# Turning half of the token layer's input with VectorE block transposes and transfers instead of TensorE

## The chip, the cores and the metric

The kernel runs on one core of one Trainium2 chip. Its time is the device time of one execution in microseconds (us); lower is better. TensorE is called PE, its weight loads PEld, VectorE DVE, ScalarE ACT, GpSimd POOL, and SyncE, which issues nearly all DMA transfers here, SP. Each of them works through its own queue in order.

## The reference

Eight batch rows are computed, each by a thresholded attention over 8 heads (576 tokens, 64 channels a head) and then an MLP mixer. Everything is float32.

```python
def _attn_ref(q, k, v, tau):                      # q, k, v: (8, 8, 576, 64)
    scale = 1.0 / np.sqrt(q.shape[-1])
    scores = scale * np.matmul(q, k.transpose(0, 1, 3, 2))
    thresh = np.max(scores, axis=-1, keepdims=True) - tau
    scores = np.where(scores >= thresh, scores, -1000000000.0)
    scores = scores - np.max(scores, axis=-1, keepdims=True)
    attn = np.exp(scores)
    attn = attn / (np.sum(attn, axis=-1, keepdims=True) + 1e-09)
    return np.matmul(attn, v).astype(np.float32)

def _moe_ref(x, w_tok1, w_tok2, w_ch1, w_ch2):    # x: (8, 576, 512), the heads side by side
    xt = x.transpose(0, 2, 1)
    h = np.maximum(xt @ w_tok1, 0.0) @ w_tok2     # over tokens: 576 -> 256 -> 576
    u = x + h.transpose(0, 2, 1)
    h2 = np.maximum(u @ w_ch1, 0.0) @ w_ch2       # over channels: 512 -> 1536 -> 512
    return (u + h2).astype(np.float32)
```

## The kernel before, in words

**Attention.** The heads are taken in pairs, `pairs` (four a row), and pairs in quads of two: four heads, half of a row's 512 channels. A quad's tokens are cut into nine units of 128 scores' rows, 18 units a row; two units make a round. For a round PE computes the scores (L777), DVE the maxima (L794), POOL a bias from them (L800), ACT the threshold (L810) and the exponential with its sum (L820), DVE the inverse (L276, L277) and POOL the scaling (L285). The result `e` has to be turned before it can meet the values. In row 0 PE does that (L300). From row 1 on DVE turns blocks of 32x32 (L315, `turn_blocks`) and four transfers on SP put the blocks where they belong (L327, `move`). Three units form a group, for which PE multiplies by the values (L365, L370, `values`) into `xT`, the attention's output with channels on partitions: `xT` is 128 partitions x 4 pairs x 576 tokens. ACT or DVE copies it out of PSUM (L374).

**Token MLP.** `token_mlp(b)` builds its steps for a row when the row's last value group has been issued. The first token layer contracts over tokens, so x is needed with tokens on partitions, in `x_sb` (128 partitions x 5 token tiles x 512 channels, one buffer for all rows; the fifth tile has 64 tokens). `turn_x` transposes 128x128 blocks of `xT` on PE into a PSUM bank (L399), `turned_x` copies the bank to `x_sb` (L403, ACT, or DVE where that one is free first). `tok1` then multiplies with `w1`, five matmuls for each of the two blocks of 128 hidden channels (L411); L416 or L419 apply the relu. `tok2` (L424) is the second token layer, and `add_x` (L435) adds its result to `xT`, which from then on holds u. For row 0 the steps are made by half rows, `token_mlp(0, range(2))` as soon as its first quad is there.

**Channel MLP.** It works on groups of 256 tokens: `ch1` (L885, relu at L890 or L893) and `ch2` (L901, added to the turned u at L915 and stored at L925). Two groups of row 0 and one of each later row but the last are done while the attention of the next row runs; they are PE's filler there. What is left of u is spilled to DRAM (L483) and taken up at the end, from L1244 on, with no attention beside it.

**What sets the order.** The program is written out by a list scheduler at build time (`Scheduler`). Each operation has an engine, a cost, dependencies and a rank; the scheduler takes for each engine the operation that can start first by its own clocks and, among those that can start at once, the one of the lowest rank. Ranks: maxima -1 or 0, transfers of `e` 0, PSUM copies 0 or 1, token steps 1.5, channel steps 2, turns of `e` 4. Score rounds after row 0 are held back until the filler of a plan has been issued (`planned_at`, with `TOKENS` and `GROUP` as PE time of a row's token and channel work). Loads of q and k for a pair (`make_pair`, L106) have rank 0. During the attention PE shares two PSUM banks for everything but the scores. While the first 110 us of the scheduler's clock last, `keep_warm` (L599) fills PE's waits with spare transposes.

**Other names.** `extra` is a buffer of 4 KB a partition, which the conversion of the weights uses during rows 0 and 1 (`load_piece`, `converted`). `HQ`, in the new code, is 2, the pairs of a quad; `NI` is 4, `MAIN` 512 and `LAST` 64 tokens. `rows_due` holds rows whose token steps are to be made, `xreads` what must be finished before `xT`'s buffer is taken by the next row but one.

Of the kernel before, what the change touches and what calls it, by code (L numbers as in the profile page):

```python
# [21 lines left out]
def kernel(  # L22
# [356 lines left out]
    class Step:  # L379


        def __init__(self, kind, cost, on, cost_out, work, leave, other=None):
            self.kind, self.cost, self.on, self.cost_out, self.work, self.leave = kind, cost, on, cost_out, work, leave
            self.other = other

    def token_mlp(b, ps=range(NP)):

        xT = xTs[b]
        L = len(ps)
        cols = slice(P * ps[0], P * ps[0] + P * L)  # L390
        n = NI // L

        def turn_x(bank, t, n):
            M = MT[t]
            to = bank[0:M, 0 : n * L * P].rearrange("p (t c x) -> p t c x", t=n, c=L)
            for i in range(n):
                for c in range(L):
                    tok = (t + i) * P
                    nc.tensor.transpose(out=to[:, i, c, :], in_=xT[:, ps[c], tok : tok + M], identity=ident)  # L399

        def turned_x(bank, t, n, copy=nc.scalar.copy):
            M = MT[t]
            copy(  # L403
                out=x_sb[0:M, t : t + n, cols], in_=bank[0:M, 0 : n * L * P].rearrange("p (t c x) -> p t (c x)", t=n, c=L)
            )

        def tok1(bank, m):
            if b not in hidden:
                hidden[b] = work.tile([P, NTK, DM], F32, tag="a", bufs=1, name=f"a_{b}")
            for t in range(NT):  # L410
                nc.tensor.matmul(  # L411
                    bank[:, 0 : P * L], lhsT=w1[:, t, P * m : P * m + P], rhs=x_sb[:, t, cols], start=(t == 0), stop=(t == NT - 1)
                )

# [23 lines left out]
        for t, n in [(t, n) for t in range(0, NI, n)] + [(NI, 1)]:  # L438
            steps.append(
                Step(  # L440
                    "x",
                    0.115 * n * L,
                    "act",
                    0.49,
                    lambda bank, t=t, n=n: turn_x(bank, t, n),
                    lambda bank, t=t, n=n: turned_x(bank, t, n),
                    ("dve", 0.61, lambda bank, t=t, n=n: turned_x(bank, t, n, nc.vector.tensor_copy)),
                )
            )
# [70 lines left out]
    class Scheduler:  # L520
# [78 lines left out]
        def keep_warm(self, t):  # L599
# [3 lines left out]
            n = int((t - now - WARM_GAP) / WARM_TURN)  # L603
            if not banks or n < 1:
                return
# [121 lines left out]
    def make_pair(n):  # L727
        b, p = pairs[n]
        if n:
            ahead = (key_op("prep", n - 2, 0), key_op("prep", n - 2, 1))  # L730
            for lo in range(0, LOADS, 2):
# [6 lines left out]
                        ahead,  # L738
                        0,
                        after=(key_op("load", n - 1, LOADS - 2),),  # L740
# [97 lines left out]
    def make_tokens(b, steps, after):  # L838

        outs = {"x": [], "1": [], "20": [], "21": []}  # L840
        for i, step in enumerate(steps):
# [3 lines left out]
            elif step.kind == "1":  # L845
                deps += outs["x"] + tokens_x.get("2", []) + [key_op("pool", 0), key_op("pool", 1), key_op("pool", 2)]
            else:
                deps += outs["1"] + [key_op("pool", j) for j in range(3, 7)]
            x, y = put_step(("tok", b, id(step)), step, deps, b)
            outs[step.kind].append(y)  # L850
            fills[b] = fills.get(b, 0.0) + step.cost
        return outs

    state = {"ch2": [], "stores": [], "adds": []}

    def make_groups(b, halves):
# [124 lines left out]
    def make_row(b):  # L981
# [9 lines left out]
        outs = halves["20"] + halves["21"]  # L991
        xreads[b] = make_groups(b, halves) + outs
        if b < B - 1:
# [32 lines left out]
    def make_round(it):  # L1026
# [28 lines left out]
        for u in us:  # L1055
# [39 lines left out]
            if t % GU == GU - 1:  # L1095
                make_group(b, p0, t // GU)
                if p0 == NP - 2 and t // GU == 2:
                    rows_due.append(b)

    rows_due = []  # L1100

# [5 lines left out]

    TOKENS, GROUP = 18.8, 41.8

# [18 lines left out]
    def grow():  # L1128

        nonlocal made  # L1130
        while made < ROUNDS and (made < 2 or key_op("S", made - 2).end is not None):
            make_round(made)
            for n in range(2, len(pairs)):
                if last_round(n - 2) == made:
                    make_pair(n)
            made += 1
        if made > 4 and not first_half and key_op("V", 2).end is not None:
            make_half_row()
# [284 lines left out]
```

## Time and profile before

| | |
|---|---|
| median of 3 runs | 1273.56 us (1271.95 to 1276.34) |
| the profiled execution | 1275.34 us |
| its span, first to last instruction | 1273.5 us |
| granted TensorE clock, mean | 0.995 |
| busy: PE, PEld, DVE, ACT, POOL | 98%, 78%, 58%, 45%, 25% |
| turning transposes (L399) on PE | x160, from 76.7 to 865.8 us |
| first token layer (L411) on PE | x180 records: 140 of 512 columns, 40 of 256 |
| PE from the end of row 7's token phase on (905 to 1273.5 us) | 363.3 of 368.5 us busy |
| transfers of `e` (L327) | x504, 144 KB each, 2.9 us to landing |

A float32 matmul of the program stands in the trace as two records, a transpose as one. Busy times count overlapping records once; mean durations don't, and a matmul's end is modelled, so the distance between the starts of successive records says more of its cost than its duration. A line of a group reads: source line, engine, operation, what it writes and reads, shapes, count, then busy time and mean duration, then the idle time of its engine ahead of it and what ended it. A line of the timeline reads: start, length, engine, source line, operation, and in brackets the idle time before it.

### The profile page before, as it was taken

How to read it: one execution, taken by the hardware profiler on the slowest of the kernel's cores; microseconds unless marked ns; L12 is line 12 of the kernel's file. 1: busy time of each engine (PE TensorE's matmuls, PEld its weight loads, DVE VectorE, ACT ScalarE, POOL GpSimd, SP SyncE). 2: the span in 40 equal slices, each digit the busy share in tenths (PEclk: the TensorE clock that was granted, in tenths of full speed). 3: DMA queues.
4: the chain of work that ended last, by engine and by line, in shares of the span. 5: the costliest groups of instructions: out<-in, count | busy, mean ns of one | idle time of the engine just before them, and what ended most of it. 6: DMA issues, size and time to landing. Idle time of an engine off the chain costs nothing.

```text
span 1273.5 us, 21544 instructions
## 1 busy us (share of the span) xinstructions
PE 1244.8 (98%) x8090; PEld 993.5 (78%) x8090; DVE 744.7 (58%) x1145; ACT 570.7 (45%) x1244; POOL 316.9 (25%) x518
## 2 busy tenths in 40 slices
PE   8889999999999999999999999999999999999998
PEld 7656778687658767876876776787988888888887
DVE  6699982574666666765766667561443534444443
ACT  6988863663655565554565467431120202011120
POOL 3665641232223332332233333210001010000100
PEclk9899999999999999999999999999999999999999
DMA  8646985356877676677676676550111101020011
GB/s 161 143 123 166 226 197 122 79 128 154 174 155 168 144 154 148 149 161 160 157 150 152 153 158 157 129 130 11 52 24 66 34 25 42 18 67 25 25 34 33
DMA packets 307191, 145.09 MB, mean 114 GB/s; under 512 B 206672, under 2 KB 299856, under 8 KB 307088
## 3 DMA queue, kind: packets, MB, share of 16 engines
q1 hardware_dynamic: 305216, 143.51, 49.0%
q8 instruction: 64, 1.05, 0.3%
q10 hardware_dynamic: 1872, 0.21, 0.1%
q14 instruction: 39, 0.32, 0.1%
HBM read 47.32 MB, written 13.50 MB: 48 GB/s over the span
## 4 chain that ended last, share of the span: by engine, by line
PE 80%; DVE 6%; SPq 4%; DMA 3%; ACT 2%; issue 1%; POOL 0%; DVEq 0%; POOLq 0%
PE bank L901 12%; PE o L1244 10%; PE bank L885 10%; PE sc L777 9%; PE bank L370 8%; PE hx L1244 6%; PE bank L411 5%; PE bank L424 4%; PE hz L1244 4%; PE oz L1244 4%; PE hmm L1244 4%; DVE mx L794 3%; PE bank L365 2%; SPq L327 2%; DMA lv<-in_v_dram 1%
## 5 line engine op out<-in xcount | busy, mean ns | idle before, releaser
L285 POOL TENSOR_SCALAR e<-e,rr 128x576 f32<-128x576 f32 x288 | 213.7, 761 | 278.1 <-DVE rr L277 263.6
L810 ACT ACTIVATE e<-sc,bias 128x576 f32<-128x576 f32 x288 | 193.8, 740 | 149.5 <-POOL bias L800 146.3
L820 ACT ACTIVATE e<-e,ntau 128x576 f32<-128x576 f32 x288 | 220.5, 777 | 0.3
L794 DVE TENSOR_REDUCE mx<-sc 128x2 f32<-128x1152 f32 x144 | 187.9, 1345 | 48.3 <-PE sc L777 48.1
L315 DVE STREAM_TRANSPOSE T<-e 128x1152 f32<-128x1152 f32 x126 | 170.6, 1363 | 47.4 <-POOL e L285 24.3
L901 PEld LDWEIGHTS bank<-wc,g 128*128 128x128 f32 x1536 | 177.7, 192 | 9.8 <-issue 5.2
L901 PE MATMUL bank<-wc,g 128*128 128x128 f32 x1536 | 181.6, 276 | 0.4 <-DVE us L915 0.3
L885 PE MATMUL bank<-xT,wc 128*128 128x256 f32 x768 | 177.2, 384 | 1.1 <-DVE g L893 0.9
L777 PE MATMUL sc<-kT,qT 64*128 64x192 f32 (+1 forms) x1920 | 169.0, 338 | 2.7 <-ACT e L810 2.7
L777 PEld LDWEIGHTS sc<-kT,qT 64*128 64x128 f32 (+1 forms) x1920 | 141.0, 179 | 33.7 <-issue 17.7
L885 PEld LDWEIGHTS bank<-xT,wc 128*128 128x128 f32 x768 | 142.0, 190 | 29.0 <-issue 6.3
L370 PE MATMUL bank<-eT,lv 128*64 128x384 f32 (+1 forms) x1024 | 136.2, 408 | 0.0
L1327 POOL TENSOR_TENSOR us<-us,ut 128x256 f32<-128x256 f32 x27 | 22.5, 847 | 391.9 <-DVE us L1165 391.9
L370 PEld LDWEIGHTS bank<-eT,lv 128*64 128x64 f32 x1024 | 74.4, 138 | 51.4 <-issue 44.7
L800 POOL TENSOR_SCALAR bias<-mx,toff 128x2 f32<-128x2 f32 x144 | 39.4, 275 | 219.7 <-DVE mx L794 213.0
L411 PE MATMUL bank<-x_sb,w 128*128 128x512 f32 (+1 forms) x180 | 72.6, 552 | 0.3 <-DVE eT L305 0.2
L424 PE MATMUL bank<-w,a 128*128 128x192 f32 (+1 forms) x256 | 72.6, 418 | 0.1
L890 ACT ACTIVATE g<-bank 128x256 f32<-128x256 f32 x67 | 25.7, 383 | 91.2 <-PE bank L885 91.0
L1292 ACT ACTIVATE ga<-hmm 128x256 f32<-128x256 f32 x30 | 11.5, 383 | 117.1 <-PE hmm L1244 117.1
L1165 DVE TENSOR_TENSOR temps<-hx,temps 128x256 f32<-128x256 f32 x60 | 25.1, 418 | 56.7 <-PE hx L1244 56.6
L820 ACT ACTIVATION_READ_ACCUMULATOR e<-e,ntau 128x1 f32 x288 | 58.2, 202 | 0.0
L411 PEld LDWEIGHTS bank<-x_sb,w 128*128 128x128 f32 x180 | 33.1, 190 | 31.9 <-issue 29.8
(131 smaller groups left out, 1532.4 us busy)
## 6 DMA issues: line engine op xcount, KB each, us to landing
eT<-T SPq DMA_DIRECT2D x504, 144.0 KB, 2.9
lk<-in_k_dram SPq DMA_DIRECT2D x126, 72.0 KB, 3.0
lq<-in_q_dram SPq DMA_DIRECT2D x124, 72.0 KB, 3.1
out_dram<-us SPq DMA_DIRECT2D x32, 256.0 KB, 2.1
ut<-us SPq DMA_DIRECT2D x128, 64.0 KB, 2.1
lv<-in_v_dram SPq DMA_DIRECT2D x112, 72.0 KB, 2.5
spare<-in_moe_w_ch_dram SPq DMA_DIRECT2D x8, 512.0 KB, 3.6
extra<-in_moe_w_ch_dram SPq DMA_DIRECT2D x8, 512.0 KB, 3.9
```

What stands on the lines that cost most here:

```text
L285: nc.gpsimd.tensor_scalar(out=eh, in0=eh, scalar1=rr[:, h : h + 1], scalar2=1.0, op0=ALU.mult, op1=ALU.mult)
L315: nc.vector.transpose(out=T.rearrange("p a (c x) -> p c a x", c=NK), in_=e.rearrange("p (c a x) -> p c a x", c=NK, a=4))
L370: nc.tensor.matmul(to[r], lhsT=lv[:, j, :], rhs=e[j], start=False, stop=(c == NI - 1), skip_group_check=True)
L411: nc.tensor.matmul(bank[:, 0 : P * L], lhsT=w1[:, t, P * m : P * m + P], rhs=x_sb[:, t, cols], start=(t == 0), stop=(t == NT - 1))
L424: nc.tensor.matmul(bank[:, n * i : n * i + n], lhsT=hidden[b][:, m, P * c : P * c + P], rhs=w2[:, m, lo : lo + n], start=(m == 0), stop=(m ...
L777: nc.tensor.matmul(sc[h][rows, f, HT * k : HT * k + HT], lhsT=qT[r, cols], rhs=kT[r, HT * f : HT * f + HT], start=True, stop=True, skip_gr ...
L794: nc.vector.tensor_reduce(out=mx[:, h], in_=sc[h][:, :, 0 : 2 * HT].rearrange("p f (k x) -> p k f x", k=2), axis=AX.XY, op=ALU.max)
L810: nc.scalar.activation(out=eh, in_=part[h], func=AF.Prelu, bias=bias[:, h], scale=SCALE, alpha=STEEP)
L820: nc.scalar.activation(out=eh, in_=eh, func=AF.Exp, bias=ntau, accum_out=rs[:, h, 0:1])
L885: nc.tensor.matmul(bank[:, 0:n], lhsT=wc1[:, j, c, :], rhs=uT[:, c, GR * i : GR * i + n], start=(c == 0), stop=(c == NCC - 1))
L901: nc.tensor.matmul(to, lhsT=s["g"][:, j, P * t : P * t + P], rhs=wc2[:, j, P * c : P * c + P], start=(j == 0 and b > 0), stop=(j == NJ - 1 ...
L1244: nc.tensor.matmul(ps, lhsT=l, rhs=r, start=start and x == 0, stop=x == len(pairs) - 1, skip_group_check=not start)
```

## The change

From row 1 on the first quad's half of x no longer passes through PE. When the value group that ends the first quad has been issued, in mid-row, `make_early(b)` lays down: two turns on DVE (`turn_main`, one for each pair: 128 channels x 512 tokens by blocks of 32x32 into `extra`), four transfers on SP (`move_main`, each from 32 partitions of `extra` to 64 columns of all 128 partitions and four token tiles of `x_sb`), one more turn for the last 64 tokens (`turn_rest`) and four transfers for it (`move_rest`). The transfers wait for the turns and for the first token layer of the row before. The channels of this half stand in `x_sb` in another order, by blocks of 32, and `tok1` reads them back in the right one.

In `token_mlp` only the second quad is turned by PE: two groups of four transposes and one of two, where there were five groups of four. For that reason `tok1` makes two products of 256 columns in one bank in place of one of 512. Row 0 is made by half rows as before.

Besides, loads of q and k from pair 4 on get rank 1 instead of 0, `TOKENS` goes from 18.8 to 17.8, and `keep_warm` no longer acts while PE's clock is at 0, which drops the ten spare transposes before the first scores.

```diff
+    HQ = NP // 2
+
+    def early_x(b):
+        xT = xTs[b]
+        main = extra.bitcast(F32).rearrange("q (a t c d) -> q a t c d", a=4, t=NI, c=HQ)
+        rest = extra.bitcast(F32)[:, 0 : 2 * HQ * 32].rearrange("q (a c d) -> q a c d", a=2, c=HQ)
+        def turn_main(c):
+            nc.vector.transpose(
+                out=main[:, :, :, c, :].rearrange("q a t d -> q t a d"),
+                in_=xT[:, c, 0:MAIN].rearrange("q (t r a) -> q t a r", t=NI, a=4),
+            )
+        def turn_rest():
+            nc.vector.transpose(
+                out=rest.rearrange("q a c d -> q c a d"), in_=xT[:, 0:HQ, MAIN:S].rearrange("q c (r a) -> q c a r", a=2)
+            )
+        def move_main(i):
+            nc.sync.dma_start(
+                out=x_sb[:, 0:NI, 32 * HQ * i : 32 * HQ * i + 32 * HQ],
+                in_=main[32 * i : 32 * i + 32].rearrange("q a t c d -> q a (t c d)"),
+            )
+        def move_rest(i):
+            nc.sync.dma_start(
+                out=x_sb[0:LAST, NI, 32 * HQ * i : 32 * HQ * i + 32 * HQ],
+                in_=rest[32 * i : 32 * i + 32].rearrange("q a c d -> q a (c d)"),
+            )
+        return turn_main, turn_rest, move_main, move_rest
+
     def token_mlp(b, ps=range(NP)):
...
-        n = NI // L
+        turned = ps[HQ:] if b else ps
+        K = len(turned)
+        to_cols = slice(P * turned[0], P * turned[0] + P * K)
+        n = NI // K
...
         def tok1(bank, m):
...
-            for t in range(NT):
-                nc.tensor.matmul(
-                    bank[:, 0 : P * L], lhsT=w1[:, t, P * m : P * m + P], rhs=x_sb[:, t, cols], start=(t == 0), stop=(t == NT - 1)
-                )
+            if K == L:
+                products = [(cols, lambda t: x_sb[:, t, cols])]
+            else:
+                first = lambda t: x_sb[:, t, 0 : P * HQ].rearrange("p (i c d) -> p c i d", i=4, c=HQ)
+                products = [(slice(0, P * HQ), first), (to_cols, lambda t: x_sb[:, t, to_cols])]
+            for at, x in products:
+                to = bank[:, at.start - cols.start : at.stop - cols.start]
+                for t in range(NT):
+                    nc.tensor.matmul(
+                        to,
+                        lhsT=w1[:, t, P * m : P * m + P],
+                        rhs=x(t),
...
-            if not banks or n < 1:
+            if not banks or n < 1 or not now:
...
                         lambda lo=lo: load_qk(n, (nc.sync,) * 2, range(lo, lo + 2)),
                         ahead,
-                        0,
+                        1 if n >= NP else 0,
...
             elif step.kind == "1":
-                deps += outs["x"] + tokens_x.get("2", []) + [key_op("pool", 0), key_op("pool", 1), key_op("pool", 2)]
+                deps += outs["x"] + early.get(b, []) + tokens_x.get("2", []) + [key_op("pool", 0), key_op("pool", 1), key_op("pool", 2)]
...
+    def make_early(b):
+        turn_main, turn_rest, move_main, move_rest = early_x(b)
+        have = [key_op("X", rank_of_group(b, 0, g)) for g in range(3)]
+        free = early.get(b - 1, converted)
+        turns = [sched.op("dve", 1.1, lambda c=c: turn_main(c), have + free, 2) for c in range(HQ)]
+        before = [x for k, x in keyed.items() if k[0] == "tok" and k[1] == b - 1 and len(k) == 3 and x.first_layer]
+        moved = [sched.op("sp", 1.2, lambda i=i: move_main(i), turns + before, 0, dmas=(1, 131, 0.645)) for i in range(4)]
+        last = sched.op("dve", 0.35, turn_rest, moved, 2)
+        moved += [sched.op("sp", 0.6, lambda i=i: move_rest(i), [last] + before, 0, dmas=(1, 16, 0.6)) for i in range(4)]
+        early[b] = moved
+        xreads.setdefault(b, []).extend(turns + [last])
...
-    TOKENS, GROUP = 18.8, 41.8
+    TOKENS, GROUP = 17.8, 41.8
...
+        while early_due and key_op("V", rank_of_group(early_due[0], 0, 2)).end is not None:
+            make_early(early_due.pop(0))
```

More of the change, by code (lines that the diff above doesn't have):

```diff
@@ L390, in token_mlp @@
         cols = slice(P * ps[0], P * ps[0] + P * L)
-        n = NI // L
+        turned = ps[HQ:] if b else ps
+        K = len(turned)
+        to_cols = slice(P * turned[0], P * turned[0] + P * K)
+        n = NI // K
         def turn_x(bank, t, n):
             M = MT[t]
-            to = bank[0:M, 0 : n * L * P].rearrange("p (t c x) -> p t c x", t=n, c=L)
+            to = bank[0:M, 0 : n * K * P].rearrange("p (t c x) -> p t c x", t=n, c=K)
             for i in range(n):
-                for c in range(L):
+                for c in range(K):
                     tok = (t + i) * P
-                    nc.tensor.transpose(out=to[:, i, c, :], in_=xT[:, ps[c], tok : tok + M], identity=ident)
+                    nc.tensor.transpose(out=to[:, i, c, :], in_=xT[:, turned[c], tok : tok + M], identity=ident)
         def turned_x(bank, t, n, copy=nc.scalar.copy):
@@ L403, in turned_x @@
             copy(
-                out=x_sb[0:M, t : t + n, cols], in_=bank[0:M, 0 : n * L * P].rearrange("p (t c x) -> p t (c x)", t=n, c=L)
+                out=x_sb[0:M, t : t + n, to_cols], in_=bank[0:M, 0 : n * K * P].rearrange("p (t c x) -> p t (c x)", t=n, c=K)
             )
@@ L409, in tok1 @@
                 hidden[b] = work.tile([P, NTK, DM], F32, tag="a", bufs=1, name=f"a_{b}")
-            for t in range(NT):
-                nc.tensor.matmul(
-                    bank[:, 0 : P * L], lhsT=w1[:, t, P * m : P * m + P], rhs=x_sb[:, t, cols], start=(t == 0), stop=(t == NT - 1)
-                )
+            if K == L:
[10 more added lines that the diff above has]
+                        rhs=x(t),
+                        start=(t == 0),
+                        stop=(t == NT - 1),
+                        skip_group_check=len(products) > 1,
+                    )
         def relu(bank, m):
@@ L441, in token_mlp @@
                     "x",
-                    0.115 * n * L,
+                    0.115 * n * K,
                     "act",
@@ L849, in make_tokens @@
             x, y = put_step(("tok", b, id(step)), step, deps, b)
+            x.first_layer = step.kind == "1"
             outs[step.kind].append(y)
@@ L854 @@
     state = {"ch2": [], "stores": [], "adds": []}
+    early = {}
+    def make_early(b):
[9 more added lines that the diff above has]
+        xreads.setdefault(b, []).extend(turns + [last])
     def make_groups(b, halves):
@@ L991, in make_row @@
         outs = halves["20"] + halves["21"]
-        xreads[b] = make_groups(b, halves) + outs
+        xreads[b] = xreads.get(b, []) + make_groups(b, halves) + outs
         if b < B - 1:
@@ L1096, in make_round @@
                 make_group(b, p0, t // GU)
-                if p0 == NP - 2 and t // GU == 2:
-                    rows_due.append(b)
-    rows_due = []
+                if t // GU == 2:
+                    (rows_due if p0 == NP - 2 else early_due).append(b)
+    rows_due, early_due = [], []
     def planned_at(row, k):
```

## The prediction

> **What bounds the kernel now.** I read the page first: busy time and the slices.
>
> ```profile
> PE 1244.8 (98%) x8090; PEld 993.5 (78%) x8090; DVE 744.7 (58%) x1145; ACT 570.7 (45%) x1244; POOL 316.9 (25%) x518
> ...
> PE   8889999999999999999999999999999999999998
> ...
> DVE  6699982574666666765766667561443534444443
> ```
>
> PE is full from the fourth slice to the end; no other engine is near it. Since a busy PE need not be a limiting PE, I then cut the span at the first turning transposes of each row (rows 1 to 6 start theirs at 225, 346, 455, 557, 660 and 762 us) and looked at single stages.
>
> ```profile
> core 0: us, PE busy (x) PEld busy (x) DVE busy (x) ACT busy (x) POOL busy (x), PEclk, DMA share, GB/s
> 224.00:346.00 122.00, 119.73 (x888) 91.74 (x884) 75.18 (x98) 71.41 (x158) 34.92 (x62) 1.00 0.60 134
> 346.00:455.00 109.00, 106.05 (x767) 79.47 (x764) 68.17 (x100) 58.48 (x126) 33.75 (x58) 0.98 0.71 159
> 455.00:557.00 102.00, 101.08 (x747) 76.53 (x747) 68.69 (x98) 57.04 (x123) 30.48 (x54) 1.00 0.68 152
> 557.00:660.00 103.00, 102.72 (x762) 78.42 (x759) 67.95 (x98) 56.71 (x123) 30.22 (x54) 1.00 0.70 156
> ```
>
> PE idles 2.3, 3.0, 0.9 and 0.3 us of these stages and VectorE about a third of each. So PE work taken out of a row shortens the row, and work given to VectorE or to the transfers is free until it makes PE wait. What PE waits for now (list of waits, 224 to 906 us):
>
> ```profile
> PE bank L365 <- DVE xT L435: 2.5, 1, 2.5
> PE bank L365 <- DMA lq<-in_q_dram: 1.6, 1, 1.6
> PE bank L365 <- DMA eT<-T: 0.9, 1, 0.9
> ```
>
> The five lines below these name the short ones; the whole list is 7.5 us. The two longest are single halts, where the order of the work happens to fall badly.
>
> **Step 1, transposes removed from PE.** A row has 20 now (16 of 128 columns wide, 4 for the last 64 tokens), in five groups of four, each with one PSUM eviction at L403; it will have 10, in groups of 4, 4 and 2. Seven rows: 70 fewer transposes, 14 fewer groups. The mean duration of one (279 ns) isn't what it costs, since they overlap. Row 1's timeline on PE:
>
> ```profile
> 225.52 0.66 PE L399 MATMUL bank<-ident,xT 128*128 128x128 f32 x4
> 226.02 1.89 PE L885 MATMUL bank<-xT,wc 128*128 128x256 f32 x8
> 227.75 0.60 PE L399 MATMUL bank<-ident,xT 128*128 128x128 f32 x4
> 228.63 1.99 PE L885 MATMUL bank<-xT,wc 128*128 128x256 f32 x8 [0.28 <-DVE g L893]
> ```
>
> From the start of a group to the start of what follows is 0.50 us in the first and 0.88 us in the second, where what follows waits for a bank. Single starts lie 0.109 us apart. I added start-to-next-start over all 35 groups of rows 1 to 7: 3.4, 3.2, 3.5, 2.9, 3.3, 2.8 and 2.2 us, 21.2 us, or 0.607 us a group. At that price the new row costs 2 x 0.607 + (0.607 - 2 x 0.109) = 1.60 us, seven rows 11.2 us: a gain of 10.0 us. Lower bound: only the bare starts go, 70 x 0.109 = 7.6 us. Upper bound: all waits behind the groups go too, and 0.109 x 10 x 7 = 7.6 us remain: a gain of 13.6 us. I take 10.0, since the waits come with groups and two groups of five go.
>
> The Trainium skill (TensorE: Matmul & The Clock Gate, Part 4) gives about 275 ns for a 128x128 PE transpose inside a kernel, close to the recorded durations; 70 of them would be 19.3 us by that page, against 7.6 us by the starts.
>
> **Step 2, the first token layer.** A full-width product (five matmuls of 512 columns) becomes two of 256. PE runs each f32 matmul as two records, so 140 records of 512 columns become 280 of 256. Ten of 512 start at 867.59 and are followed at 871.88: 0.429 each. Eight of 256 columns (L885 above) take 226.02 to 227.75: 0.216 each. The change is 280 x 0.216 - 140 x 0.429 = +0.4 us. By mean busy time per record it is more:
>
> ```profile
> L411 PE MATMUL bank<-x_sb,w 128*128 128x512 f32 x140 | 63.1, 599 | 0.0
> ...
> L411 PE MATMUL bank<-x_sb,w 128*128 128x256 f32 x40 | 9.4, 387 | 0.3 <-DVE eT L305 0.2
> ```
>
> 280 x 9.4/40 - 63.1 = +2.7 us, the upper bound. The weight loads grow with the matmuls, from 180 to 320 records, but at 190 ns each they stay under the 216 ns of the matmul they hide behind, as L885's do. The right-hand side of the first product is read in runs of 32 columns; the values matmuls (L370) read eT so from row 1 on and start 0.316 us apart per pair of 384 columns, the same in row 0 where the columns are dense. I take +0.4.
>
> **Step 3, added on VectorE.** Two turns of 128x512 and one of 128x128 a row. The nearest row is the residual's turn, same 512 elements with the same stride of four:
>
> ```profile
> L870 DVE STREAM_TRANSPOSE us<-xT 128x512 f32<-128x512 f32 x12 | 12.7, 1096 | 16.2 <-DMA out_dram<-us 16.2
> ```
>
> 2 x 1.10 + 0.27 (the only 128x128 turn, L492) = 2.5 us a row, 17 us in all, against some 33 us of idle VectorE in each row; a few of the 14 evictions that go (0.68 us each on VectorE) come off again. They are issued in mid-row with a worse rank than the maxima (L794) and a better one than the turns of e (L315). Queued behind them are the turns of e, whose transfers feed the values (L365); those have PE filler in front, the channel matmuls. Cost nothing; with that cover gone, up to 2.5 us a row.
>
> **Step 4, added transfers.** Eight issues a row on SP: four of 128 KB (512 pieces of 256 B) and four of 16 KB. SP issues one in about 0.65 us (four eT moves take 2.52 to 2.66 us), 8 x 0.65 = 5.2 us a row, and in 224 to 906 us it sat waiting 200 us, some 29 us a row. Landing, by the nearest transfers:
>
> ```profile
> eT<-T SPq DMA_DIRECT2D x504, 144.0 KB, 2.9
> lq<-in_q_dram SPq DMA_DIRECT2D x124, 72.0 KB, 3.1
> ut<-us SPq DMA_DIRECT2D x128, 64.0 KB, 2.1
> lv<-in_v_dram SPq DMA_DIRECT2D x112, 72.0 KB, 2.5
> ```
>
> lq comes in 576 pieces of 128 B, so 3 us is near; by eT's bytes 2.9 us, and twice lv's 288 pieces would be 5 us. They are needed half a row later (some 50 us), when tok1 runs; hidden, though tok1 now waits on PE for their landing too, with all of PE's queue behind it. Each transfer waits for the VectorE turn and stands in front of eT moves, q/k loads and v loads; if an eT move comes late it is L365 that waits. The Trainium skill (DMA: Bandwidth & Descriptors, Specifications) asks for 512 B or more per piece; the trace agrees in so far as lv's 72 KB in 256 B pieces took 2.5 us, ut's 64 KB in 512 B pieces 2.1 us.
>
> **Step 5, order.** q/k loads of later pairs drop behind the eT moves, pacing is tightened by 1.0 us a row, and from row 1 on the order of fillers shifts a little on all engines. The 7.5 us of PE's waits sit where the order falls badly, so they may go or double: -7.5 to +7.5 us; I take 0, the amount of channel matmuls between score rounds being nearly what it was. The 10 warming transposes before the first scores go: those scores start at 8.27 us behind the turn of q that ends at 8.09, so nothing.
>
> **Sum.** -10.0 + 0.4 = -9.6 us. The profiled execution took 1275.3 us (span 1273.5 and 1.8 around it), 1.8 over the median of 1273.56; so 1265.7 for an execution like it, 1264.0 for the median. The unknown terms give -13.6 + 0.4 - 7.5 = -20.7 to -7.6 + 2.7 + 7.5 = +2.6: 1253 to 1276.
>
> **Rivals.** *A, a full duration each.* If a removed transpose frees its 279 ns, the gain is 70 x 0.279 = 19.5 us less 0.4: 1254.5. For it: the groups followed by waits (0.88 us for four) come near it. Against: row 7's five groups take 0.44 us each, four starts and nothing more. The Trainium skill's figure in step 1 would give the same case.
> *B, the gain is handed back.* Tighter pacing and three instead of five short PE pieces leave less to fill the ends of the token phase, where transposes, evictions and tok1 depend on each other; row 2's 20 transposes ran without filler, 3.2 us. New waits as large as the old 7.5 us, and tok1 at its upper 2.7 us: -10.0 + 2.7 + 7.5 = +0.2, 1274. Against it: PE has had 0.9 us or less of idle time in rows 3 to 6.
> *C, SP's queue delays the values: slower.* In row 2 PE stood before L365 from 362.62 to 365.63 us and then ran at half clock until 369: starts of the next five were 0.63 instead of 0.32 apart, so 3.0 + 1.6 = 4.6 us. If the eight extra transfers in front of eT moves made such a halt once a row, that is 7 x 4.6 - 9.6 = +22.6, 1296; it decides from 9.6/4.6, two to three halts, on, and four give 1282. For it: the transfers land in mid-row among the eT moves, DMA share is already 0.7. Against: SP's 29 us of waiting a row, over five times the addition.
> *D, the old halts go as well:* -9.6 - 7.5 = -17.1, 1256.5.
>
> **Chances.** Forecast 0.62, its own range 1258 to 1269; A 0.05, D 0.12, B 0.13, C 0.08. 0.3% is 3.8 us, about what a measurement of this kernel can tell from no change, so faster ends at 1269.7: forecast, A and D, less 0.01 for the forecast's upper edge, make 0.78; B and that edge 0.14 for no change; C 0.08 for slower. Range 1254 to 1276: it leaves out C alone.
>
> **What would show it.** 90 turning transposes on PE in place of 160, group to next start still 0.4 to 0.9 us. 320 records in the first token layer in place of 180, all of 256 columns and 0.216 us apart. VectorE's new turns 1.1 us each in mid-row. Row windows about 1.4 us shorter each with PE as full as now. Wrong: PE idle of more than 10 us between 224 us and the end of the rows (B or C; C if it stands before L365 with a late eT), or new transfers landing after tok1 wants them.

## The result and the profile after

| | before | after |
|---|---|---|
| median (lowest to highest) of 22 runs each | 1273.92 us (1271.23 to 1277.80) | 1270.75 us (1264.36 to 1276.59) |
| ratio to before, 95% interval | | 0.9973 [0.9962, 0.9985] |
| the profiled execution, its span | 1275.34, 1273.5 us | 1273.39, 1271.4 us |
| mean granted clock, profiled execution | 0.995 | 0.991 |
| end of the rows' token phases | 905.3 us | 903.0 us |

The change saves 3.4 us by the ratio, 0.27%, about a third of the 9.6 us forecast; the interval lies clear of 1. The page after, busy time and slices:

```profile
PE 1237.8 (97%) x8150; PEld 1015.3 (80%) x8150; DVE 755.0 (59%) x1163; ACT 564.0 (44%) x1233; POOL 315.4 (25%) x518
...
PE   8888999999999999999989999999999999999998
...
DVE  6699982656666667756666756761443534444443
```

PE is busy 7.0 us less than before and is still the bound. But there is a new 8 in PE's 21st slice, and PE's share fell from 98 to 97%: part of what was saved turned into waiting. Groups of PE and VectorE after (line, busy time, mean ns, idle time ahead):

```profile
L435 PE MATMUL bank<-ident,xT 128*128 128x128 f32 (+1 forms) x90 | 14.5, 279 | 1.7 <-ACT x_sb L439 1.0 <-DVE eT L305 0.7
...
L454 PE MATMUL bank<-x_sb,w 128*128 128x256 f32 x320 | 72.8, 383 | 0.3 <-DVE eT L305 0.2
...
L395 DVE STREAM_TRANSPOSE extra<-xT 128x512 f32<-128x512 f32 x14 | 15.3, 1112 | 0.0
...
L401 DVE STREAM_TRANSPOSE extra<-xT 128x128 f32<-128x128 f32 x7 | 2.2, 308 | 10.5 <-DMA eT<-T 6.2 <-DMA x_sb<-extra 3.3 <-issue 1.0
```

L435 is the old L399: 90 transposes for 160. L454 is the old L411: 320 records, all of 256 columns. The turns on VectorE take 1.11 and 0.31 us. All that is as laid out. The new transfers (KB each, us to landing):

```profile
x_sb<-extra SPq DMA_DIRECT2D x28, 128.0 KB, 3.2
...
x_sb<-extra SPq DMA_DIRECT2D x28, 16.0 KB, 1.9
```

What is new stands in the list of PE's waits (224 to 906 us):

```profile
PE bank L948 <- ACT g L953: 5.1, 3, 2.6
PE bank L365 <- DMA x_sb<-extra: 1.9, 1, 1.9
PE bank L365 <- DVE xT L483: 1.0, 1, 1.0
```

L948 is the first product of the channel MLP (L885 before), which had waited 0.9 us for its relu before. It now stands still in rows 5 and 6. (The halt of L365, at 339 us, is taken up under the rivals.) The timeline of row 5, in order of time, with the lines between left out:

```profile
619.55 2.09 SPq L406 DMA_DIRECT2D x_sb<-extra  x2
...
620.44 0.25 DVE L978 TENSOR_TENSOR us<-bank,ut 128x128 f32<-128x128 f32 x1
...
621.75 0.66 SPq L531 DMA_DIRECT2D spill<-xT  x1
...
622.50 6.47 SPq L327 DMA_DIRECT2D eT<-T  x8
...
629.08 2.48 SPq L412 DMA_DIRECT2D x_sb<-extra  x4
...
630.89 2.22 PE L825 MATMUL sc<-kT,qT 64*128 64x192 f32 x24
...
631.60 0.59 SPq L988 DMA_DIRECT2D out_dram<-us  x1
...
634.41 2.08 DVE L933 STREAM_TRANSPOSE us<-xT 128x512 f32<-128x512 f32 x2 [3.95 <-DMA out_dram<-us]
...
636.42 1.33 DVE L315 STREAM_TRANSPOSE T<-e 128x1152 f32<-128x1152 f32 x1
637.68 2.58 DVE L842 TENSOR_REDUCE mx<-sc 128x2 f32<-128x1152 f32 x2
...
639.09 0.27 POOL L848 TENSOR_SCALAR bias<-mx,toff 128x2 f32<-128x2 f32 x1 [5.53 <-DVE mx L842]
639.39 1.37 ACT L858 ACTIVATE e<-sc,bias 128x576 f32<-128x576 f32 x2 [3.94 <-POOL bias L848]
...
640.65 0.39 ACT L953 ACTIVATE g<-bank 128x256 f32<-128x256 f32 x1
...
641.09 3.55 PE L948 MATMUL bank<-xT,wc 128*128 128x256 f32 x8 [2.60 <-ACT g L953]
```

Read it as a chain. The store of the row before (L988) has its data at 620.69, when the last addition L978 ends. It is issued at 631.60, because SP issues transfers without a break from 619.55 on, turning transfers (L406, L412) among them; L412's four, 2.48 us, stand right in front of it. The store frees `us`, which has one buffer, so VectorE's residual turn L933 waits 3.95 us. Behind it in VectorE's queue stand the maxima L842 of scores that PE began at 630.89. The threshold L858 waits for their bias, and behind L858 in ScalarE's queue stands the relu L953, which frees PE's bank. PE stands for 2.60 us, and then eight records take 3.55 us instead of the 1.9 of the same lines elsewhere. Windows over that place (busy time and count of PE, PEld, DVE, ACT and POOL, then the granted clock, the DMA share and GB/s):

```profile
630.90:637.40 6.50, 6.50 (x46) 5.79 (x45) 2.99 (x3) 0.92 (x3) 2.66 (x4) 1.00 0.51 108
637.40:640.80 3.40, 1.08 (x6) 0.60 (x4) 3.34 (x6) 1.41 (x3) 0.53 (x2) 1.00 0.64 128
640.80:644.20 3.40, 3.11 (x7) 2.52 (x8) 1.49 (x2) 3.40 (x8) 0.00 (x0) 0.51 0.70 179
644.20:647.60 3.40, 3.40 (x30) 2.73 (x29) 1.55 (x4) 1.11 (x4) 1.69 (x3) 0.99 0.82 180
```

The halt is followed by 3.4 us at half clock. The Trainium skill (TensorE: Matmul & The Clock Gate, Part 1) puts half speed after an idle window of about 3.4 us; the length of the slow stretch agrees, but here PE had still been busy for 1.08 us of the 3.4 before it. The same chain runs in row 6: L412 at 734.69, store at 737.22, L933 after 3.95 us idle, L948 after 2.08 us, half clock from 746.7 to 750.1. The row 6 of the kernel before, at the same place:

```profile
733.86 0.54 SPq L925 DMA_DIRECT2D out_dram<-us  x1
...
737.30 2.12 DVE L870 STREAM_TRANSPOSE us<-xT 128x512 f32<-128x512 f32 x2 [0.55 <-DMA out_dram<-us]
...
739.61 2.22 PE L777 MATMUL sc<-kT,qT 64*128 64x192 f32 x24
```

The turn waits 0.55 us there and PE not at all.

To see both sides of the balance I took the distances between successive starts on PE, records that start within 20 ns of each other as one. For each pair of kinds of instruction the tenth percentile of these distances, over the three kernels of the table together, counts as usual; the sum of these over the rows is bare work, what goes beyond it is stalls (counted from 140 us on, half clock included). The end is the start of PE's last record in the rows.

| | bare work, us | stalls, us | end of the rows, us |
|---|---|---|---|
| before | 833.8 | 37.9 | 905.3 |
| after | 825.2 | 44.0 | 903.0 |
| after, early turns and transfers left out | 824.4 | 30.5 | 886.9 |

This is an estimate: with another percentile the levels move by many microseconds. The differences hardly do. From before to after the work fell by 8.6 us (8.6 to 8.8 with any percentile from 5 to 40) and the stalls rose by 6.1 (6.1 to 6.3). Two halts, at 638 and 744 us, make 4.7 and 4.1 us of after's stalls. The third line is the first experiment.

### The profile page after: what moved, and what is told of

Its sections match the earlier page's. It is cut to its first block, busy times and chain, and to the rows that moved or that the text cites. A ratio compares the mean times of both kernels' runs of the same rounds, so it can differ in the third digit from the quotient of the medians.

```text
span 1271.4 us, 21773 instructions
## 1 busy us (share of the span) xinstructions
PE 1237.8 (97%) x8150; PEld 1015.3 (80%) x8150; DVE 755.0 (59%) x1163; ACT 564.0 (44%) x1233; POOL 315.4 (25%) x518
## 4 chain that ended last, share of the span: by engine, by line
PE 78%; SPq 6%; DVE 5%; DMA 5%; ACT 4%; issue 2%; POOL 0%; DVEq 0%; ACTq 0%; POOLq 0%
PE bank L964 11%; PE bank L948 10%; PE o L1309 10%; PE sc L825 9%; PE bank L370 7%; PE hx L1309 6%; PE bank L454 5%; PE hmm L1309 4%; PE oz L1309 4%; PE hz L1309 4%; PE bank L472 4%; SPq L327 3%; PE bank L365 2%; DVE mx L842 2%; ACT e L858 2%
## 5 line engine op out<-in xcount | busy, mean ns | idle before, releaser
L858 ACT ACTIVATE e<-sc,bias 128x576 f32<-128x576 f32 x288 | 194.1, 740 | 156.8 <-POOL bias L848 155.1
L842 DVE TENSOR_REDUCE mx<-sc 128x2 f32<-128x1152 f32 x144 | 188.1, 1347 | 58.9 <-PE sc L825 58.4
L948 PE MATMUL bank<-xT,wc 128*128 128x256 f32 x768 | 181.0, 389 | 6.1 <-ACT g L953 5.1
L948 PEld LDWEIGHTS bank<-xT,wc 128*128 128x128 f32 x768 | 144.2, 192 | 36.6 <-ACT g L953 6.5
L454 PE MATMUL bank<-x_sb,w 128*128 128x256 f32 x320 | 72.8, 383 | 0.3 <-DVE eT L305 0.2
L454 PEld LDWEIGHTS bank<-x_sb,w 128*128 128x128 f32 x320 | 59.8, 190 | 11.3 <-issue 1.3
L953 ACT ACTIVATE g<-bank 128x256 f32<-128x256 f32 x66 | 25.3, 383 | 92.9 <-PE bank L948 92.7
```

Source lines behind the costliest of these rows:

```text
L454: nc.tensor.matmul(to, lhsT=w1[:, t, P * m : P * m + P], rhs=x(t), start=(t == 0), stop=(t == NT - 1), skip_group_check=len(products) > 1,)
L842: nc.vector.tensor_reduce(out=mx[:, h], in_=sc[h][:, :, 0 : 2 * HT].rearrange("p f (k x) -> p k f x", k=2), axis=AX.XY, op=ALU.max)
L858: nc.scalar.activation(out=eh, in_=part[h], func=AF.Prelu, bias=bias[:, h], scale=SCALE, alpha=STEEP)
L948: nc.tensor.matmul(bank[:, 0:n], lhsT=wc1[:, j, c, :], rhs=uT[:, c, GR * i : GR * i + n], start=(c == 0), stop=(c == NCC - 1))
```

## The experiments

My theory (Q in the texts below) was that the eight transfers hand back most of the gain through SP's queue. The rivals: VectorE's turns do it by themselves (V), the edits of the order do it (O), or the transposes were simply worth less (P). Gains below are (1 - ratio) x 1273.9 us; by the intervals each is uncertain by 1.5 to 3 us, a difference of two by 3 to 4.

**Leaving out the early turns and transfers, or the transfers alone.** The order of all other instructions is unchanged.

```diff
-        turns = [sched.op("dve", 1.1, lambda c=c: turn_main(c), have + free, 2) for c in range(HQ)]
+        turns = [sched.op("dve", 1.1, lambda: None, have + free, 2) for c in range(HQ)]
...
-        moved = [sched.op("sp", 1.2, lambda i=i: move_main(i), turns + before, 0, dmas=(1, 131, 0.645)) for i in range(4)]
-        last = sched.op("dve", 0.35, turn_rest, moved, 2)
-        moved += [sched.op("sp", 0.6, lambda i=i: move_rest(i), [last] + before, 0, dmas=(1, 16, 0.6)) for i in range(4)]
+        moved = [sched.op("sp", 1.2, lambda: None, turns + before, 0, dmas=(1, 131, 0.645)) for i in range(4)]
+        last = sched.op("dve", 0.35, lambda: None, moved, 2)
+        moved += [sched.op("sp", 0.6, lambda: None, [last] + before, 0, dmas=(1, 16, 0.6)) for i in range(4)]
```

> The changed kernel with the early turns on VectorE and their eight transfers left out (from row 1 on the first quad's half of x in the token layer is stale); the order of everything else is untouched. Theory Q (the PE part is worth its 9.6 us, and SP's extra transfers hand back some 6 us by delaying the store that the residual turn L933 waits for): 1263 to 1265, 9 to 11 us under before, no PE halt over 2 us ahead of L948 in late rows. Rival V (VectorE's extra turns hand it back): the same here. Rival P (the PE part itself is worth only 3 to 4 us): 1270, like the changed kernel.

Measured: 1257.94 us, 0.9875 [0.9854, 0.9897], a gain of 15.9 us, more than theory or rivals had. The second kernel keeps the turns (`turn_main`, `turn_rest`) and empties the transfers only.

> The changed kernel with VectorE's early turns kept and all eight transfers a row left out (the first quad's half of x is stale from row 1 on). Theory Q: 1263 to 1266, as with nothing early at all, and the idle time of VectorE ahead of L933 falls under 8 us from 17.4. Rival V: 1269 to 1271, as the changed kernel.

Measured: 1258.30 us, 0.9873 [0.9851, 0.9894], 16.2 us. So VectorE's turns cost nothing that shows, V and P are out, and the transfers hand back 15.9 - 3.4 = 12.5 us. The rest of the change is worth more than the forecast had; where that comes from stands in the section on the prediction.

**The four small transfers left out** (`lambda: None` in the line of `move_rest`).

> The changed kernel without the four small transfers a row (L412; x of the last 64 tokens of the first quad is stale from row 1 on). They stand right ahead of the store L988 in rows 5 and 6 and take SP 2.5 us. Theory Q: most of the halts go, 1264 to 1267. Rival V, and a variant of Q in which the four large transfers matter: 1269 to 1271.

Measured: 1263.96 us, 0.9915 [0.9893, 0.9937], 10.8 us: 7.4 more than after. Row 5 of this kernel:

```profile
625.51 0.60 SPq L988 DMA_DIRECT2D out_dram<-us  x1
...
627.27 2.22 PE L825 MATMUL sc<-kT,qT 64*128 64x192 f32 x24
...
628.84 2.11 DVE L933 STREAM_TRANSPOSE us<-xT 128x512 f32<-128x512 f32 x2 [1.99 <-DMA out_dram<-us]
...
632.14 2.57 DVE L842 TENSOR_REDUCE mx<-sc 128x2 f32<-128x1152 f32 x2
...
635.54 1.99 PE L948 MATMUL bank<-xT,wc 128*128 128x256 f32 x8 [0.68 <-ACT g L953]
```

Store, turn, maxima and PE's wait move together, and without the half clock the eight records take 1.99 us.

**The store ahead of the transfers**, by the rank of the store.

```diff
-                stores.append(sched.op("sp", 0.35, lambda t=t, f=store: f(t), outs, 2, dmas=(1, 150, 0.35)))
+                stores.append(sched.op("sp", 0.35, lambda t=t, f=store: f(t), outs, -1, dmas=(1, 150, 0.35)))
```

> The whole changed kernel, but the stores of finished channel groups get rank -1 in place of 2, so that SP issues them ahead of loads and moves that could start at the same time. Theory Q: L933 waits under 8 us in all, the halts ahead of L948 go, 1263 to 1267. Rivals V and P: unchanged, 1269 to 1272.

Measured: 1268.42 us, 0.9950 [0.9930, 0.9971], 6.4 us, 3.0 more than after, between the ranges of Q and of its rivals. The halts at 638 and 744 us are gone, but others stand at 338 to 342, 425, 447 and 770. What is taken from the front of the queue for the store may come late elsewhere; this run doesn't show it, since the order of the other engines changes in it too and the profiled execution, at 1273.20 us, was the slowest of its eleven.

**An eighth of the bytes** in the large transfers, as many issues.

```diff
-                out=x_sb[:, 0:NI, 32 * HQ * i : 32 * HQ * i + 32 * HQ],
-                in_=main[32 * i : 32 * i + 32].rearrange("q a t c d -> q a (t c d)"),
+                out=x_sb[0:16, 0:NI, 32 * HQ * i : 32 * HQ * i + 32 * HQ],
+                in_=main[32 * i : 32 * i + 4].rearrange("q a t c d -> q a (t c d)"),
```

> The changed kernel with its eight transfers a row in their places, but each of the four large ones carries an eighth of its bytes (4 of 32 source partitions; most of the first quad's half of x is stale from row 1 on). Theory Q-place (it is the place and time that the transfers take on SP's queue): 1268 to 1271, as the changed kernel. Rival Q-data (it is the bytes, and with them the landing that later transfers and VectorE's last early turn wait for): 1262 to 1265, near what is left when the large ones are gone.

Measured: 1264.54 us, 0.9931 [0.9908, 0.9954], 8.8 us: 5.4 more than after, as the rival had it. So the number of issues isn't the whole cost; what the large transfers move counts too. The order is the same on every engine, so row 5 can be laid beside after's:

```profile
615.14 1.46 SPq L406 DMA_DIRECT2D x_sb<-extra  x2
...
617.39 6.13 SPq L327 DMA_DIRECT2D eT<-T  x8
...
626.15 0.59 SPq L988 DMA_DIRECT2D out_dram<-us  x1
...
626.50 2.22 PE L825 MATMUL sc<-kT,qT 64*128 64x192 f32 x24
...
635.25 2.00 PE L948 MATMUL bank<-xT,wc 128*128 128x256 f32 x8 [1.14 <-ACT g L953]
```

The same two issues of L406 take 1.46 us here and 2.09 in after, the eight of `eT` behind them 6.13 and 6.47. With full bytes single issues on SP become longer: the first of these two takes 1.41 us in after and 0.71 here, and in row 6 one issue of `eT` takes 2.04 and 0.60. Measured from the start of the scores, the store goes out 1.1 us sooner than in after in row 5 and 2.4 us sooner in row 6. So in these two profiles a good part of what the bytes cost comes through the same chain: they delay SP itself.

**The transfers behind the residual's turn of the row before** (rank 3, and `after` that turn).

```diff
+    held = {}
...
-        moved = [sched.op("sp", 1.2, lambda i=i: move_main(i), turns + before, 0, dmas=(1, 131, 0.645)) for i in range(4)]
+        moved = [sched.op("sp", 1.2, lambda i=i: move_main(i), turns + before, 3, after=(held.get(b - 1),), dmas=(1, 131, 0.645)) for i in range(4)]
...
+                held[b] = turn
```

> The whole changed kernel, but the early transfers may go only once the residual turn of the row before has been laid down, and with rank 3 in place of 0, so that on SP they stand behind the store that this turn waits for. Theory Q-place: 1259 to 1265, and VectorE idles less than 12 us ahead of L933, PE less than 4 us between 224 us and the end of the rows. Rival Q-data or any cost that comes with the transfers wherever they stand: 1268 to 1271.

Measured: 1278.25 us, 1.0048 [1.0031, 1.0065]: slower than before. VectorE's wait for the store falls as it should, from 17.4 us to:

```profile
DVE us L934 <- DMA out_dram<-us: 3.2, 2, 1.8
```

But PE now halts at 337 and at 385 to 390 us, and again at 398 and 776; at the second L365 waits 4.84 us while SP issues eight `eT` transfers behind the first L406. Of this miss I can say that the order of the whole program moved, not which edit of it made these halts.

**The small transfers replaced by PE.** The last 64 tokens of the first quad are turned by PE with the second quad's: 14 transposes more than after.

```diff
+            chans = ps if t == NI else turned
+            C = len(chans)
...
-        last = sched.op("dve", 0.35, turn_rest, moved, 2)
-        moved += [sched.op("sp", 0.6, lambda i=i: move_rest(i), [last] + before, 0, dmas=(1, 16, 0.6)) for i in range(4)]
```

> The whole changed kernel, with the last 64 tokens of the first quad turned by PE as before, so that the third turn and the four small transfers a row go. PE gets two transposes a row back, 14 x 0.109 = 1.5 us. Theory Q: leaving these transfers out gave 1264.0, so 1264 to 1267. Rival (that run gained by the output's missing part in some other way): 1269 to 1272.

Measured: 1265.68 us, 0.9941 [0.9919, 0.9963], 7.5 us, 4.1 more than after. Four transfers a row cost more here than two transposes on the engine that bounds the kernel, though some of the order on all engines changes with the edit.

**The transfers issued by ScalarE's queue.**

```diff
-            nc.sync.dma_start(
+            nc.scalar.dma_start(
...
-        moved = [sched.op("sp", 1.2, lambda i=i: move_main(i), turns + before, 0, dmas=(1, 131, 0.645)) for i in range(4)]
+        moved = [sched.op("act", 0.65, lambda i=i: move_main(i), turns + before, 0, dmas=(1, 131, 0.645)) for i in range(4)]
```

> The whole changed kernel, with the eight transfers a row issued from ScalarE's queue in place of SP's; same bytes, same time of the row. Theory Q-place: SP is as free as before, 1260 to 1266, if ScalarE (44% busy) finds room for 5 us of issues a row; where it doesn't, its relus and thresholds come late and PE waits for L953 or L858. Rival Q-data: 1268 to 1272.

Measured: 1296.35 us, 1.0187 [1.0161, 1.0213], far outside both ranges. An issue takes about as long as on SP. What it holds up is not shown: the order on all engines changes with this edit, and PE's longest waits in the rows name loads of v (7.4 us), VectorE's additions L483 (5.1 us) and its PSUM copies (2.9 us), while the relus ahead of L948 come to 1.3 us and thresholds don't appear.

**The order edits alone**, in the kernel before.

```diff
-            if not banks or n < 1:
+            if not banks or n < 1 or not now:
...
-                        0,
+                        1 if n >= NP else 0,
...
-    TOKENS, GROUP = 18.8, 41.8
+    TOKENS, GROUP = 17.8, 41.8
```

> The kernel before with only the three small edits of the change: loads of q and k from pair 4 on at rank 1, TOKENS at 17.8, no spare transposes before the first scores. Leaving out all early work gave 16 us, 6 more than the 9.6 us of step 1 and 2. Theory O (these 6 us are the new order, which happens to fall better): 1266 to 1270. Rival (they belong to the halved transposes and evictions, with their waits): 1272 to 1276.

Measured: 1271.48 us, 0.9979 [0.9966, 0.9992], 2.7 us, between the two ranges. In the new kernel with the loads' rank set back to 0:

> The whole changed kernel with the loads of q and k back at rank 0. Theory Q-place, with SP's queue full in mid-row: more transfers ahead of the stores and moves, 1270 to 1278. Rival O' (the rank has nothing to do with it): 1269 to 1272.

Measured: 1276.52 us, 1.0022 [1.0009, 1.0036]. There the rank of the loads is worth 2.8 + 3.4 = 6.2 us. That fits a fuller queue, in which what stands in front counts for more; but the order of PE, VectorE and ScalarE changes as well, so the reason isn't shown.

**The small transfers issued later**, behind the residual's transfers (L940) of the row before; nothing else moves.

```diff
+    def behind(b, f):
+        if b < 3 or b - 1 in residual:
+            f()
+        else:
+            waiting.setdefault(b, []).append(f)
...
-        moved += [sched.op("sp", 0.6, lambda i=i: move_rest(i), [last] + before, 0, dmas=(1, 16, 0.6)) for i in range(4)]
+        moved += [sched.op("sp", 0.6, lambda i=i: behind(b, lambda: move_rest(i)), [last] + before, 0, dmas=(1, 16, 0.6)) for i in range(4)]
...
+                if k == 3:
+                    residual.add(b)
+                    for f in waiting.pop(b + 1, []):
+                        f()
```

A first form had no exception for the early rows, so that in row 2 these transfers came after the token layer that reads them:

> The whole changed kernel in its own order, but for one thing: the four small transfers of a row are written out behind the residual's transfers (L940) of the group that runs meanwhile, so that they no longer stand ahead of the store which VectorE's residual turn waits for. Bytes and issues are the same, and PE's order is the same. Theory Q-place: close to the run without these transfers, 1263 to 1267, the halts ahead of L948 in rows 5 and 6 fall from 2.6 and 2.1 us to 1.2 or less. Rival (their issue or landing costs wherever they stand): 1269 to 1272.

Measured: 1267.18 us, 0.9940 [0.9920, 0.9961]. The form shown:

> The whole changed kernel in its own order, with the four small transfers a row written out behind the residual's transfers from row 3 on; in rows 1 and 2 they stay, since there the residual's transfers come after the token layer. Same bytes and issues, PE's order the same. Theory Q-place: 1264 to 1268, no halt over 1.5 us ahead of L948 in rows 5 and 6. Rival (place doesn't matter, the issues and bytes cost wherever they stand): 1269 to 1272.

Measured: 1267.32 us, 0.9948 [0.9929, 0.9967], 6.6 us: 3.2 more than after with the same transfers and bytes. Row 5 (L940 and L959 are after's L933 and L948):

```profile
629.52 0.59 SPq L999 DMA_DIRECT2D out_dram<-us  x1
...
631.57 2.22 PE L825 MATMUL sc<-kT,qT 64*128 64x192 f32 x24
...
633.46 2.10 DVE L940 STREAM_TRANSPOSE us<-xT 128x512 f32<-128x512 f32 x2 [2.31 <-DMA out_dram<-us]
...
636.75 2.57 DVE L842 TENSOR_REDUCE mx<-sc 128x2 f32<-128x1152 f32 x2
...
640.15 1.99 PE L959 MATMUL bank<-xT,wc 128*128 128x256 f32 x8 [0.98 <-ACT g L964]
```

Measured from the start of the scores, the store goes out 2.8 us sooner than in after, the turn starts 1.6 us sooner, and PE's wait is 1.6 us shorter. From the start of the scores to that of the maxima pass 6.79 us (after, row 5), 6.28 (after, row 6), 5.31 (an eighth of the bytes), 5.18 (here) and 4.87 (small transfers left out); PE waits 2.60, 2.08, 1.14, 0.98 and 0.68 us. Each time it is the delay less 4.2 us: the chain has that much slack in this order and no more.

**The large transfers deferred likewise**, with the last tokens on PE.

> The whole computation: the last 64 tokens of the first quad on PE as in e7_rest_on_pe, and the four large transfers written out behind the residual's transfers. No early transfer then stands ahead of a store. Theory Q-place: below e7 (ratio 0.9941), at 1258 to 1264, 1.5 us over what PE's added transposes allow at best. Rival (bytes cost wherever they are): as e7, 1264 to 1268.

Measured: 1276.12 us, 1.0012 [0.9999, 1.0025]. Not a clean test: the transfers were issued too late for the token layer. In row 2 it waited for them; in row 6 its first half ran before they were issued, so without them, and the second waited (L457 is its matmul here):

```profile
PE bank L457 <- DMA x_sb<-extra: 12.4, 2, 8.3
```

**Longer pieces.** As with the last tokens on PE, and `x_sb` laid out so that a large transfer writes 128 pieces of 1024 B in place of 512 of 256 B. The engines' order is the same as without it.

```diff
+    x_flat = x_sb.rearrange("p t x -> p (t x)")
...
-                out=x_sb[:, 0:NI, 32 * HQ * i : 32 * HQ * i + 32 * HQ],
+                out=x_flat[:, MAIN // 2 * i : MAIN // 2 * i + MAIN // 2],
...
```

> As e7_rest_on_pe (the last 64 tokens on PE, no small transfers, the order of all engines the same), but the early half of x lies by blocks in x_sb, so that a large transfer writes 128 pieces of 1024 B in place of 512 of 256 B. If the large transfers cost by the time that their pieces keep the DMA engines (18 ns for 256 B; a 1152 B piece takes 51, so 128 of 1024 B some 6 us of engine time in place of 9), 1261 to 1264, and landing under 3.0 us from 3.2. If they cost by their place on SP's queue alone: 1264 to 1267, as e7 (ratio 0.9941).

Measured: 1263.32 us (1259.72 to 1266.59), 0.9916 [0.9896, 0.9937], 10.7 us, the lowest median of the kernels that turn the whole of x. Its landing, and its store and turn in row 5 (L943 is after's L933):

```profile
x_sb<-extra SPq DMA_DIRECT2D x28, 128.0 KB, 2.8
```

```profile
624.08 0.54 SPq L998 DMA_DIRECT2D out_dram<-us  x1
...
627.38 2.18 DVE L943 STREAM_TRANSPOSE us<-xT 128x512 f32<-128x512 f32 x2 [0.33 <-DMA out_dram<-us]
```

Landing is 0.4 us shorter than the 3.2 of the kernel with 256 B pieces, and in row 5 the turn finds its buffer nearly free (idle 0.33 us, 1.39 with 256 B pieces). In row 6 it doesn't: the turn waits 2.59 us for the store, PE 2.14 us ahead of its first channel product, and half clock follows; with 256 B pieces PE waits 1.62 us there. At the same order the kernel with 256 B is 3.2 us slower, but the two intervals overlap, so that longer pieces save time is not shown.

## Why the prediction was wrong

The direction was right, the size was not: 3.4 us for 9.6.

**Step 1 (transposes) came out near its size.** By the measure of the prediction, start of a group to the start of what follows, the 140 transposes of rows 1 to 7 took 21.2 us before. The 70 that are left take 12.3 us after, and 12.6 with the early work left out: 8.7 to 8.9 us gained, between the lower bound of 7.6 and the 10.0 taken. The waits behind the groups did not all go.

With the transfers left out the kernel gains 16.2 us all the same. The bare work fell by 9.4 us there, by the table; the other 7.4 us are stalls. The largest part of these are two halts in the profile of the kernel before: L365 at 340 us (1.62 us) and at 366 us (2.52 us, with half clock behind it) make some 6 us of its stalls. With the early work left out PE has no wait of 0.9 us or more from 200 us to the end of the rows. So what came on top of steps 1 and 2 looks mainly like what rival D named, the old halts going as well, for which it had 1256.5 us. The order edits alone bring 2.7 us; how the rest divides between order and lighter work is not shown.

**Step 2 held:** 320 records, and single starts lie 0.216 us apart, also where the operand is read in runs of 32 columns.

**Step 3 held:** 2 x 1.11 + 0.31 = 2.5 us a row on VectorE, and the kernel with the turns alone is no slower than the one without (16.2 and 15.9 us gained).

**Step 4 is the step that failed: "hidden".** The median issue (0.63 and 0.60 us) and the landing (3.2 us) came out as worked out, and yet the transfers hand back 12.5 us, for which neither the sum nor the range had a term. The argument was SP's 29 us of waiting a row. After the change the ten largest entries of SP's waits in the rows still sum to 144.5 us, some 20 us a row, and none of it helps: SP had no gap of more than 0.15 us from 619.55 to 632 us, just where the transfers go. Nor is the median what an issue costs there: single ones take 1.4 to 2.0 us. An average over a row said nothing of the queue at their place. I named `eT` moves and loads as what stands behind them; the store stands behind them too, and I had met the store's landing only as the wait of 16.2 us in the line of L870, which gave me the price of a turn, not as the release of a buffer that VectorE's whole queue stands behind.

How it splits: leaving out the small transfers brings back 7.4 us, of which 3.2 come from their place alone; cutting the large ones' bytes brings back 5.4. Both act on the same chain, so the parts need not add up. By the count of starts the two halts of the chain shown make 8.8 us of after's profile.

**Step 5 (order)** was given 0 within +-7.5; alone it brings 2.7 us.

**The rivals.** C named the right queue and the right form: a wait, then half clock. Its price of 4.6 us is counted from start to start and so holds 0.3 us of work; the two halts cost 4.7 and 4.1. Its victim was right once and wrong twice. The two dear halts run over store, VectorE and ScalarE to L948, not over `eT` to L365. But L365 is struck as well, at 339 us:

```profile
327.58 0.62 SPq L406 DMA_DIRECT2D x_sb<-extra  x1
...
331.20 5.52 SPq L327 DMA_DIRECT2D eT<-T  x8
336.82 2.48 SPq L412 DMA_DIRECT2D x_sb<-extra  x4
...
339.41 0.87 PE L365 MATMUL bank<-eT,vl 128*64 128x384 f32 x4 [1.88 <-DMA x_sb<-extra]
```

L365 reads `eT`, and the last of those eight transfers is issued from 336.1 to 336.7 us; with the 3.0 us that `eT` takes to land by the median it is there at 339.1 to 339.7, when L365 starts, so I take `eT` for what it waits for. In the kernels without the transfers, of the same order, there is no such wait; with the small ones left out it is 3.35 us. C reckoned with one halt a row; there were three in all, and since the old ones went, the change still gained. B's 1274 is nearer the median than the forecast's 1264.0, but its place, the ends of the token phase, is not where the time went. The sign that I had set for a wrong forecast was met: the row windows from 225.9 to 903.0 us have PE busy for 665.4 of 677.1 us, 11.7 idle, where it had been 7.7.

**Not every execution has the same halts.** The mean granted clock is known for each execution, and one half-clock stretch of 3.4 us lowers it by 0.5 x 3.4 / 1271 = 0.0013. Over all executions it is 0.9945 before (73), 0.9931 after (22) and 0.9955 with the early work left out (6): after has about one stretch more than before and 1.8 more than it need have. At 1.7 us for the clock and 2.1 to 2.6 for the wait, 1.8 stretches would be some 7 us of the 12.5. This is a rough estimate, since the mean holds the stretches of row 0 too, where no early transfer stands: 13.7 us of half clock in after's profile, 10.2 in the one with the early work left out. In after's 22 executions the mean goes from 0.990 to 0.998. The highest belongs to the fastest, 1264.36 us. That lies beside the forecast by luck, as the best of 22, and it is still 6.4 us over the median with the early work left out, so the clock is not all of the cost. One profile a kernel can't show which halts the others have.

**Open:** why single issues on SP become longer beside the large transfers, and whether their bytes also act through their own landing, which L401 and L412 wait for; and why the large ones, issued later, made worse halts around 337 and 385 us. A second buffer for `us`, which would cut the chain at the store, was not tried.

## What to carry to other kernels

An average of idle time says nothing of a queue that works in order: before work is added to it, lay out what it issues at that very place, what stands behind, and which single buffer that frees. When a saving on the bounding engine is paid for with transfers, cost each transfer also by the slack of the chain behind it (here 4.2 us), and count with up to 1.7 us more for a halt of 2 us and over, as half clock may follow. A last remainder left on the bounding engine gave more here than moving everything off it.

## What was unexpected of the hardware

- A wait of 2.08 us on PE was enough for 3.4 us at half clock (granted clock 0.50), PE having been busy for 1.3 of the 3.4 us before. A wait of 2.99 us, in the kernel with the small transfers issued later, had none. What tells them apart is where they fall: in each kernel's trace all half-clock stretches between 0 and 905 us start whole multiples of 3.413 us apart. Divide the rows of all sixteen traces (130 to 905 us) into these windows: of those at full clock, the 20 in which PE was busy for 0.40 or less were each followed by half clock, and none of those with 0.43 or more was. The 2.08 us lay in one window (busy 0.39), the 2.99 us in two (0.56 and 0.57).
- For the same 128 KB between the same buffers, 256 B pieces took 18 ns each by the median and 1024 B pieces 46 (each over all transfers of the kernel with such pieces): 512 x 18 ns = 9.2 us of DMA engines' time against 128 x 46 ns = 5.9.
- An issue of the same large transfer took 0.62 to 1.41 us on SP (0.63 by the median) and 0.62 to 2.24 us on ScalarE (0.65), and one issue of `eT` on SP 2.04 us in place of 0.60: the median hides the issues that hold up a queue.
